# Shorter stages for the second layer's weight sums and a wider spread of the next token sums

## The chip, the cores and the metric

The kernel runs on one core of one Trainium2 chip. The core has TensorE (PE, the products; PEld is its weight load), VectorE (DVE), ScalarE (ACT), GpSimd (POOL) and SyncE (SP, which issues all DMAs here from one queue). Each engine works through its own queue in order. The metric is the time of one execution on the device in microseconds, the median of several runs.

## The reference, cut to what matters

Attention over four batches with eight heads (576 tokens, 64 wide), mixed with a memory read-out, gives 2304 tokens of 512 values. Two feed-forward layers follow, with 512 x 2048 weights in and 2048 x 512 out:

```python
x = attn_out.transpose(0, 2, 1, 3).reshape(B * S, H * D)
h = x @ w1_in;  x = (h * np.cos(h)) @ w1_out                            # layer one
h = x @ w2_in;  x = (h * np.tanh(np.log1p(np.exp(h)))) @ w2_out         # layer two
```

The weights come as 64-bit floats and are taken apart on the chip.

## The kernel before, in words

Every factor of the feed-forward products is split into a high and a low half in the fast 32-bit format, and a product is three matmuls: high by high, high by low, low by high.

The work runs in these stages. **Attention** (0 to about 395 us) goes through 80 steps (16 head pairs of 5 row blocks); each step has parts a, b and c, and the main loop (L840) hangs other work behind part a. **Layer one, first half** of the hidden units, runs beside attention in blocks of 256 tokens and on to about 490 us; **its second half** (`m2`, L875) runs in blocks of 512 tokens from about 490 to 690 us: 72 yields, each about twelve products of 512 columns. The chain of the cosine there goes from PE over ACT (L380), DVE (L381), ACT (L385), DVE (L388), ACT (the high half) to POOL (the low half, L398), whose result PE needs for the products of L492.

**Layer two** (`strassen_ffn`, from about 690 us) uses Strassen's scheme: seven products of sums of blocks in place of eight. It runs over 3 token blocks of 768 and, in each, over 8 groups of 256 hidden units, 24 groups in all. A group has 84 matmuls of 384 columns: 42 for the first products (`product`, L750: the seven of `PROD`) and 42 for the second products (L725), which belong to the pair of groups two earlier and go in the order of `LAST`. A group's sums are DVE's (L649, L644), the activation is ACT's (L653), the high halves are ACT's and the low halves POOL's (`halves`, L656 to L662). After the last pair of a token block, `done` (L670) forms the outputs from the seven accumulators, alternating DVE and POOL (L684), and stores them.

What layer two needs is prepared elsewhere:

- *Weight sums* (`strassen_weights`, L532). For a group, two raw pieces are fetched and converted (L143 to L146), four sums are formed on POOL (L544), and four results are split on ACT and on DVE or POOL in turn (L547, L548) and stored to DRAM (L549): 2 loads and 4 stores in SP's queue. The eight groups of the weight in are made beside attention from step 33 on (`SUM0`, `SUMR`), the eight of the weight out beside `m2`, one raw piece in four yields. The four results of a group have four buffers, `ws0`, `ws2`, `ws3`, `ws5`, one each.
- *Token sums* (`strassen_x`, L562). A token block needs seven sums of its four quarters, split. For the first block they are made beside `m2`; for the others inside `strassen_ffn`: at the end of group 6 the four loads, two differences and two of the seven splits, and in group 7 the rest, one part after each product (`coming`). DVE does differences and splits (L576, L583, L593, L598), ACT the high halves (L575).

The order on each engine comes from a planner with a model of times; `tc.issue_after(x)` keeps what is issued inside from being placed ahead of instruction x.

Of the kernel before, what the change touches and what calls it, by code (L numbers as in the profile page):

```python
# [20 lines left out]
BUFS = dict(  # L21
    mb=2, kd=4, qd=3, aD=4, vt=2, qt=1, ph=2, den=2, mo=4, xH=1, xL=3, sm=7, mn=2, at=8, aT=7, u=2, e=3, g=4, h=4, y=4, xb=3, xbH=4, xbL=4, yp=3, wst=4, S=6, T=8, sw=1, ws=1, wq=10, xr=4, xt=2, xc=9, xc0=2, us=14, g3=17, y3=6, h3=2, w2=8, ac=14,
)
# [4 lines left out]
SUM0 = 36  # L28
SUMR = 0.4
# [11 lines left out]
    wh="ap", aT="av", yl="p", ml="p", y0="v", y1="a", aD="v", y3="a", yf="vp", x3l="v", x3l0="pv", x3d0="p", x3d="v", ws4="p", ws2="a", wh2="a",  # L41
# [8 lines left out]
def attention_moe_moe_kernel(  # L50
# [140 lines left out]
    def attention(ap, pools):  # L191
# [46 lines left out]
        def stage_a(b, p, i):  # L238
# [37 lines left out]
            nc.vector.reciprocal(sm, sm)  # L276
            for j, at in enumerate(ats):
                turn_of("sc", b == 0).tensor_scalar(at[:, :N], at[:, :N], sm[:, j:j + 1], gates[j], ALU.mult, ALU.mult)  # L278
# [242 lines left out]
    LAST = "A11 A12 S2 S3 A22 S1 S4".split()  # L521
# [10 lines left out]
    def strassen_weights(srcs, order, dst):  # L532

        pc = []
        for n, t in enumerate(ahead(srcs), -AHEAD):
            if t is not None:
                pc.append(t.rearrange(f"p ({order}) -> p h c f", c=2, h=2))
            if len(pc) == 2:
                (a11, a21), (a12, a22) = [[q[:, h] for h in range(2)] for q in pc]
                sw = wk.tile([P, 4, 2, P], F32, tag="sw", name="sw", bufs=BUFS["sw"])  # L540
                s1, s2, s3, s4 = [sw[:, k] for k in range(4)]
                for d, x, y, op in ((s1, a21, a22, ALU.add), (s2, s1, a11, ALU.subtract),
                                    (s3, a11, a21, ALU.subtract), (s4, a12, s2, ALU.subtract)):
                    turn_of("ws4").tensor_tensor(d, x, y, op)  # L544
                for k0, k1, t in ((0, 2, pc[1]), (2, 3, pc[0][:, 0:1]), (3, 5, sw[:, :2]), (5, 7, sw[:, 2:])):
                    ws = wk.tile([P, k1 - k0, 2, 2, P], F32R, tag=f"ws{k0}", name="ws", bufs=BUFS["ws"])
                    scaled("wh2", ws[:, :, 0], t)  # L547
                    turn_of("w2l").tensor_tensor(ws[:, :, 1], t, ws[:, :, 0].bitcast(F32), ALU.subtract)  # L548
                    nc.sync.dma_start(dst[n // 2, :, k0:k1], ws.rearrange("p k l c f -> p k (l c f)").bitcast(F32))  # L549
                pc = []  # L550
            yield n + 1

    def strassen_in(win):
        wi = win.bitcast(I32).rearrange("(c p) (f two) -> p c f two", p=P, two=2)
        return strassen_weights([wi[:, c:c + 2, f:f + 2 * P, :] for f in range(0, DFF, 2 * P) for c in range(0, NC, 2)],
                                "c h f", wsD)

    def strassen_out(wout):
        wo = wout.bitcast(I32).rearrange("(f p) (e two) -> p f e two", p=P, two=2)
        return strassen_weights([wo[:, f] for f in range(DFF // P)], "h c f", woD)  # L560

    def strassen_x(t0, out, store=False):  # L562
# [22 lines left out]

        halves("A11", b11)
        t1 = diff(b12, b11)
        t2 = diff(b22, t1)
        halves("S2", t2)
# [3 lines left out]
        turn_of("x3d" + u).tensor_tensor(b12, b22, b12, ALU.subtract)  # L593
        halves("S3", b12)
# [3 lines left out]
        turn_of("x3d" + u).tensor_tensor(b21, b21, t2, ALU.subtract)  # L598
        halves("A22", b21)
        yield  # L600
        halves("S4", b22)

# [20 lines left out]
    def strassen_ffn(pool, xs, w, fill):  # L623
# [9 lines left out]
        g3 = wk.tile([P, BUFS["g3"], 2, TS], F32R, name="g3")  # L633
# [8 lines left out]
        def sub(x, y, out=None):  # L642
            out = cell() if out is None else out
            marks['v'] = nc.vector.tensor_tensor(out, x, y, ALU.subtract).ins  # L644
            return out
# [10 lines left out]
        def halves(k, name, x):  # L656
            slot = free.pop(0)
            t = g3[:, slot]
            scaled("mh", t[:, 0], x)
            ins = turn_of("ml").tensor_tensor(t[:, 1], x, t[:, 0].bitcast(F32), ALU.subtract).ins  # L660
            marks['p' if ins.engine == mybir.EngineType.Pool else 'v'] = ins
            g[k, name] = slot, t  # L662
# [7 lines left out]
        def done(k0, name, c, y):  # L670
# [3 lines left out]
            if tl == 0:  # L674
                a = acc[name, c] = ring(wk, "ac", [P, TS])
                scaled("y3", a, y)
                return
# [21 lines left out]
            elif name == "S2":  # L699
                pre("S3", a)  # L700
                pre("S4", a)
            elif name == "S3":
                pre("A22", a, ALU.subtract)
            elif name == "A22":
                store(a, 1, 0)
            elif name == "S1":
                pre("S4", a)
                turn_of("yf").tensor_tensor(a, a, acc["S3", c], ALU.add)
                store(a, 1, 1)
            else:  # L710
                store(a, 0, 1)

        def last_products():
            for i in range(2):
                fetch_last(i)
            for i, (k0, name) in enumerate(chain):
# [26 lines left out]
        for k in range(n + KS):  # L743
            nw = {}

            def product(b, name, first):
# [8 lines left out]
                with behind():  # L755
# [216 lines left out]
```

## Time and profile before

| what | value |
|---|---|
| median of 3 runs | 1070.65 us (1068.82 to 1073.72) |
| the profiled execution | 1071.4 us |
| its span, first to last instruction | 1069.5 us |
| mean granted TensorE clock | 0.983 |
| instructions | 19321 |

The profile is one execution. The views used below give, for a stretch of the span, how long each engine was busy and with how many instructions; for one line, its count and mean duration; and, in order of time, what ended the idle time before an instruction. A stretch in which PE runs fewer matmuls of one size than elsewhere is a stretch in which it waited.

### The profile page before, as it was taken

To read this page: it belongs to the slowest core of one execution; us is meant where nothing else is said; L and a number is where in the kernel's file an instruction comes from. 1 tells how busy PE (TensorE), PEld (TensorE's weight loads), DVE (VectorE), ACT (ScalarE), POOL (GpSimd) and SP (SyncE) were. 2 spreads that over 40 slices of the span, in tenths; PEclk is the share of its full clock that TensorE was granted. 3 is DMA by queue.
4 is the path that set the end of the run, shared out by engine and by line. 5 is a ranking of instruction groups with operands and counts; after the bars stand their busy time and mean duration, and the time that the engine had idled before them with its cause. 6 is when DMAs were issued, how large, how long until landed. Compare 5 with 4: busy or idle time off the path is not lost.

```text
span 1069.5 us, 19321 instructions
## 1 busy us (share of the span) xinstructions
PE 1021.0 (95%) x6704; PEld 901.6 (84%) x6704; DVE 704.2 (66%) x1442; ACT 580.7 (54%) x1274; POOL 597.1 (56%) x581
## 2 busy tenths in 40 slices
PE   6988999998999999999999999999989999899996
PEld 4665678886878889998887888999989999799996
DVE  3689876658566645886584784454688466973666
ACT  5787676867575743334464564554443644545441
POOL 3378736555455524654575776554547545665555
PEclk8999899999999999999999999999999999999998
DMA  7367636646552337424586798987588958687781
GB/s 251 131 215 260 191 131 199 240 160 240 177 180 107 108 118 265 151 99 128 162 296 223 273 364 314 393 296 259 198 276 260 329 205 271 218 297 254 248 288 59
DMA packets 121840, 236.18 MB, mean 221 GB/s; under 512 B 11920, under 2 KB 35984, under 8 KB 121744
## 3 DMA queue, kind: packets, MB, share of 16 engines
q1 hardware_dynamic: 121744, 234.95, 63.9%
q8 instruction: 54, 0.88, 0.3%
q14 instruction: 42, 0.34, 0.1%
HBM read 176.44 MB, written 58.46 MB: 220 GB/s over the span
## 4 chain that ended last, share of the span: by engine, by line
PE 71%; DVE 13%; DMA 6%; ACT 3%; POOL 3%; issue 3%; SPq 1%; POOLq 0%; DVEq 0%; ACTq 0%
PE h L426 16%; PE y L492 16%; PE y L725 12%; PE h L750 12%; PE o L337 5%; PE sp L251 4%; PE tp L310 3%; DVE wst L146 2%; PE o L326 1%; DMA w<-woD 1%; DMA xbH<-xsH 1%; DVE wst L145 1%; DVE us L644 1%; PE mp L290 1%; DVE xc L576 1%
## 5 line engine op out<-in xcount | busy, mean ns | idle before, releaser
L660 POOL TENSOR_TENSOR g<-us,g 128x384 fp32r<-128x384 f32 x168 | 186.1, 1128 | 144.5 <-ACT g L129 48.7
L492 PE MATMUL y<-g,w 128*128 128x256 f32 (+1 forms) x1344 | 223.9, 319 | 1.2 <-POOL g L398 1.2
L492 PEld LDWEIGHTS y<-g,w 128*128 128x128 f32 x1344 | 193.0, 192 | 28.0 <-issue 10.9
L426 PE MATMUL h<-xbH,w 128*128 128x256 f32 (+1 forms) x896 | 208.5, 318 | 0.7 <-DMA xbH<-xsH 0.7
L725 PE MATMUL y<-g,w 128*128 128x384 f32 x1008 | 199.2, 339 | 7.2 <-DMA w<-woD 3.2
L750 PE MATMUL h<-xc,wq 128*128 128x384 f32 x1008 | 197.4, 336 | 7.4 <-DVE us L649 6.0
L725 PEld LDWEIGHTS y<-g,w 128*128 128x128 f32 x1008 | 178.0, 190 | 12.1 <-DMA w<-woD 6.6
L750 PEld LDWEIGHTS h<-xc,wq 128*128 128x128 f32 x1008 | 176.5, 188 | 10.3 <-DVE us L649 7.9
L426 PEld LDWEIGHTS h<-xbH,w 128*128 128x128 f32 x896 | 151.5, 191 | 13.8 <-DMA xbH<-xsH 1.1
L398 POOL TENSOR_TENSOR g<-u,g 128x512 fp32r<-128x512 f32 x72 | 108.4, 1521 | 82.7 <-DVE g L131 54.4
L278 POOL TENSOR_SCALAR at<-at,sm,omg 128x128 f32<-128x128 f32 (+2 forms) x144 | 109.4, 769 | 73.6 <-DVE sm L276 45.8
L649 DVE TENSOR_TENSOR us<-h,us 128x384 f32<-128x384 f32 x120 | 66.4, 554 | 114.5 <-PE h L750 105.8
L426 PE MATMUL h<-xbL,w 128*128 128x256 f32 (+1 forms) x448 | 141.3, 315 | 0.0
L129 ACT ACTIVATE g<-us 128x384 fp32r<-128x384 f32 x168 | 86.6, 525 | 40.0 <-DVE us L644 37.6
L653 ACT ACTIVATE us<-us 128x384 f32<-128x384 f32 x72 | 37.9, 526 | 113.8 <-DVE us L649 107.1
L426 PEld LDWEIGHTS h<-xbL,w 128*128 128x128 f32 x448 | 85.8, 192 | 5.4 <-issue 0.3
L380 ACT ACTIVATE u<-h 128x512 int32<-128x512 f32 x72 | 42.5, 594 | 80.8 <-PE h L426 76.7
L256 ACT ACTIVATE at<-at,mn 128x128 f32<-128x128 f32 (+3 forms) x128 | 71.2, 557 | 24.0 <-DVE mn L253 22.5
L644 DVE TENSOR_TENSOR us<-us 128x384 f32<-128x384 f32 x96 | 74.8, 814 | 11.8 <-ACT us L653 9.5
L146 DVE SCALAR_TENSOR_TENSOR wst<-wst 128x512 int32<-128x512 int32 x64 | 79.2, 1247 | 0.2
L381 DVE SCALAR_TENSOR_TENSOR u<-u,h 128x512 f32<-128x512 int32 x72 | 48.4, 681 | 46.8 <-ACT u L380 46.4
L310 PE MATMUL tp<-ident,at 128*128 128x128 f32 x384 | 66.1, 289 | 9.1 <-POOL at L278 6.8
(103 smaller groups left out, 1505.2 us busy)
## 6 DMA issues: line engine op xcount, KB each, us to landing
wq<-wsD SPq DMA_DIRECT2D x168, 256.0 KB, 4.7
w<-woD SPq DMA_DIRECT2D x168, 256.0 KB, 4.9
wsD<-ws SPq DMA_DIRECT2D x24, 512.0 KB, 5.4
woD<-ws SPq DMA_DIRECT2D x24, 512.0 KB, 6.3
wst<-in_w1i_dram SPq DMA_DIRECT2D x16, 512.0 KB, 4.5
wst<-in_w1o_dram SPq DMA_DIRECT2D x16, 512.0 KB, 4.9
wst<-in_w2i_dram SPq DMA_DIRECT2D x16, 512.0 KB, 4.7
wst<-in_w2o_dram SPq DMA_DIRECT2D x16, 512.0 KB, 5.1
```

The lines of the kernel that those rows point to most:

```text
L129: eng.activation(dst, src, AF.Copy, scale=scale)
L146: nc.vector.scalar_tensor_tensor(lo, hi, 3, lo, ALU.logical_shift_left, ALU.bitwise_or)
L256: marks["act"] = nc.scalar.activation(at[:, :N], at[:, :N], AF.Exp, bias=mn[:, j:j + 1], scale=-1.0, accum_out=sm[:, j:j + 1]).ins
L278: turn_of("sc", b == 0).tensor_scalar(at[:, :N], at[:, :N], sm[:, j:j + 1], gates[j], ALU.mult, ALU.mult)
L310: nc.tensor.transpose(tp[:, c:c + P], at[:, c:c + P], ident)
L398: turn_of(kind).tensor_tensor(gL, g, gH.bitcast(F32), ALU.subtract)
L426: nc.tensor.matmul(h[:, a * T:(a + 1) * T], w_[:, c, f0:f0 + P], x_[c], start=m == 0, stop=m == 3 * NC - 1)
L492: nc.tensor.matmul(y[e // per][:, cols], w_[:, f, es], g_, start=fst and m == 0 and e % per == 0, stop=lst and m == 2, skip_group_check=True)
L644: marks['v'] = nc.vector.tensor_tensor(out, x, y, ALU.subtract).ins
L660: ins = turn_of("ml").tensor_tensor(t[:, 1], x, t[:, 0].bitcast(F32), ALU.subtract).ins
L725: nc.tensor.matmul(y, w_[:, wl, c], x[:, xl], start=m == 0, stop=m == 3 * KS - 1, skip_group_check=True)
L750: nc.tensor.matmul(b, w[name][:, wl, c], x[name][:, xl, c], start=first and m == 0, stop=m == 5, skip_group_check=True)
```

## The change

1. The weight sums go in stages. `strassen_weights` now stops after each fetch ahead, each converted raw piece, each two of the four sums, and each stored result: eight stages a group. The main loop takes one stage in each attention step from step 29 on (51 stages: three fetches and six groups), behind the step's exponential, its scaling on POOL and its reciprocal on DVE. The other ten groups (two of the weight in, eight of the weight out) go beside `m2`, once the conversion of layer one's weights is over: two stages a yield, one in each third.
2. The four result buffers become one ring of two, `ws`. The token ring `xc` has ten buffers, not nine.
3. `strassen_x` stops after every difference and split, twelve steps; in `strassen_ffn` it begins behind group 3 of a token block and takes its steps at the places in `STEPS` (group counted from the block's end, product), the loads first.
4. Layer two's second products go in the order A11, A12, S4, S1, S2, S3, A22, and `done` combines them accordingly; the subtractions for S3 and A22 go to POOL in all groups but the last, whose low halves alternate between DVE and POOL (`mz`); `h3` has three PSUM banks, `y3` five; operand slots and accumulators are tiles of their own; the first weights of the second products are fetched behind group 0.

```diff
-    ... ws=1, xc=9, y3=6, h3=2 ...
+    ... ws=2, xc=10, y3=5, h3=3 ...
-SUM0 = 36
-SUMR = 0.4
+SUM0 = 32
+SUMS = 6
+SUM2 = 3
...
-            nc.vector.reciprocal(sm, sm)
+            marks["vec"] = nc.vector.reciprocal(sm, sm).ins
...
+    STEPS = [(-4, 4), (-3, 2), (-3, 4), (-3, 6), (-2, 1), (-2, 3), (-2, 5), (-2, 6), (-1, 1), (-1, 2), (-1, 3), (-1, 5)]
-    LAST = "A11 A12 S2 S3 A22 S1 S4".split()
+    LAST = "A11 A12 S4 S1 S2 S3 A22".split()
...
+    def strassen_weights(pieces):
+        raws = ahead([src for srcs, _, _ in pieces for src in srcs])
+        for _ in range(AHEAD):
+            next(raws)
+            yield
+        for _, order, dst in pieces:
+            pc = []
+            for _ in range(2):
+                pc.append(next(raws).rearrange(f"p ({order}) -> p h c f", c=2, h=2))
+                yield
...
+                turn_of("ws4").tensor_tensor(d, x, y, op)
+                if i % 2:
+                    yield
+            for k0, k1, t in ((0, 2, pc[1]), (2, 3, pc[0][:, 0:1]), (3, 5, sw[:, :2]), (5, 7, sw[:, 2:])):
+                ws = wk.tile([P, 2, 2, 2, P], F32R, tag="ws", name="ws", bufs=BUFS["ws"])[:, :k1 - k0]
+                scaled("wh2", ws[:, :, 0], t)
+                turn_of("w2l").tensor_tensor(ws[:, :, 1], t, ws[:, :, 0].bitcast(F32), ALU.subtract)
+                nc.sync.dma_start(dst[:, k0:k1], ws.rearrange("p k l c f -> p k (l c f)").bitcast(F32))
+                yield
...
             elif name == "S2":
                 pre("S3", a)
+                turn_of("yf").tensor_tensor(a, a, acc["S1", c], ALU.add)
                 pre("S4", a)
+                store(acc["S4", c], 0, 1)
             elif name == "S3":
                 pre("A22", a, ALU.subtract)
+                pre("S1", a)
+                store(acc["S1", c], 1, 1)
             elif name == "A22":
                 store(a, 1, 0)
...
+            if k == 1:
+                next(lasts)
...
-                with behind():
-                    next(coming, None)
+                j = PROD.index(name)
+                for a in range(STEPS.count((groups[k][1] - ng, j))):
+                    with behind():
+                        next(coming, None)
...
-                halves(k, "S3", sub(r22, r12, r12))
-                halves(k, "A22", sub(t2, r21, r21))
+                halves(k, "S3", sub(r22, r12, r12, k + 1 == n))
+                halves(k, "A22", sub(t2, r21, r21, k + 1 == n))
-                if groups[k][1] == ng - 2 and k + 2 < n:
+                if groups[k][1] == ng // 2 - 1 and k + ng < n:
...
         if kind == "a" and s >= SUM0 - AHEAD:
-            with tc.issue_after(marks["act"]):
-                while summed < min(s - SUM0 + 1 if s < SUM0 else int((s - SUM0 + 1) * SUMR), DFF // P):
-                    summed = next(gi)
+            with tc.issue_after(marks["act"]), tc.issue_after(marks["pool"]), tc.issue_after(marks["vec"]):
+                next(gi, None)
...
-            if i % 4 == 1:
+            if done_b == 4 * NTL - 1:
                 with tc.issue_after(marks["cos"]), tc.issue_after(last_sin[0]):
-                    next(gc, None)
-            if i >= XSUM0 and i % 4 == 3:
+                    for _ in range(1 if i % SUM2 == 0 else 2):
+                        next(gc, None)
+            if i >= XSUM0 and i % 2 == 1:
```

## Rows read from the trace of the kernel before

**Rows 1.** The page's first part: busy us, share of span, instructions.
```profile
PE 1021.0 (95%) x6704; PEld 901.6 (84%) x6704; DVE 704.2 (66%) x1442; ACT 580.7 (54%) x1274; POOL 597.1 (56%) x581
```

**Rows 2.** Busy us (instructions) by stretch, then PE clock, DMA share, GB/s.
```profile
775.00:850.00 75.00, 69.93 (x384) 67.61 (x383) 53.30 (x83) 35.70 (x70) 43.38 (x38) 0.98 0.87 298
850.00:900.00 50.00, 50.00 (x291) 50.00 (x290) 30.11 (x51) 23.02 (x47) 28.59 (x27) 1.00 0.66 218
900.00:975.00 75.00, 69.88 (x383) 65.74 (x382) 53.31 (x82) 34.90 (x69) 44.28 (x38) 1.00 0.79 267
```

**Rows 3.** Timeline, first block change: start, us, instructions, [idle before <-releaser].
```profile
786.25 1.76 DVE L576 TENSOR_TENSOR xc<-xr,xc 128x768 fp32r<-128x768 f32 x1
...
788.06 2.37 PE L725 MATMUL y<-g,w 128*128 128x384 f32 x12 [1.14 <-DMA w<-woD]
...
799.07 1.38 PE L750 MATMUL h<-xc,wq 128*128 128x384 f32 x6 [2.22 <-DVE us L649]
```

**Rows 4.** Timeline, the end of the span.
```profile
1051.20 0.96 PE L725 MATMUL y<-g,w 128*128 128x384 f32 x4 [2.01 <-POOL g L660]
...
1052.77 10.16 PE L725 MATMUL y<-g,w 128*128 128x384 f32 x48 [0.60 <-ACT g L129]
...
1065.09 1.01 DVE L690 TENSOR_TENSOR ac<-y,ac 128x384 f32<-128x384 f32 x2
```

**Rows 5.** Busy time by stretch, beside attention.
```profile
250.00:275.00 25.00, 21.81 (x184) 18.05 (x185) 20.19 (x54) 19.04 (x48) 16.57 (x20) 1.00 0.64 226
300.00:325.00 25.00, 21.48 (x166) 16.56 (x166) 18.47 (x56) 19.28 (x48) 12.87 (x16) 0.93 0.63 220
```

**Rows 6.** Timeline beside attention, one wait of PE.
```profile
264.42 0.66 ACT L144 ACTIVATE wst<-wst 128x512 int32<-128x512 uint32 x1
...
265.39 0.65 PE L337 MATMUL o<-aT,vt 128*64 128x128 f32 x6 [1.81 <-ACT aT L129]
```

**Rows 7.** Busy time by stretch, layer one's second half and after.
```profile
521.00:590.00 69.00, 68.34 (x302) 56.27 (x301) 45.00 (x57) 36.30 (x60) 43.30 (x37) 1.00 0.72 250
590.00:654.00 64.00, 64.00 (x284) 52.98 (x283) 48.13 (x51) 38.17 (x61) 48.04 (x35) 1.00 0.83 308
654.00:700.00 46.00, 46.00 (x309) 43.80 (x308) 23.29 (x34) 23.43 (x40) 25.19 (x23) 1.00 0.95 358
```

**Rows 8.** Groups by line: total busy us, mean ns | idle before, releasers.
```profile
L660 POOL TENSOR_TENSOR g<-us,g 128x384 fp32r<-128x384 f32 x168 | 186.1, 1128 | 144.5 <-ACT g L129 48.7 <-PE y L725 39.7 <-issue 32.1
...
L644 DVE TENSOR_TENSOR us<-us 128x384 f32<-128x384 f32 x96 | 74.8, 814 | 11.8 <-ACT us L653 9.5 <-DMA wq<-wsD 0.6
...
L684 POOL TENSOR_TENSOR ac<-ac 128x384 f32<-128x384 f32 x15 | 20.8, 1399 | 16.5 <-DVE ac L690 15.0 <-PE h L750 1.3
```

**Rows 9.** Raw weights, 480 to 700 us: ns min/median/max, first, last start.
```profile
L145 DVE SCALAR_TENSOR_TENSOR wst<-wst x21: 678/683/2340, 485.3 to 673.6; 128x512 int32<-128x512 int32 x21
L146 DVE SCALAR_TENSOR_TENSOR wst<-wst x21: 675/1666/2343, 487.6 to 674.3; 128x512 int32<-128x512 int32 x21
...
L129 ACT ACTIVATE wst<-wst x16: 654/664/675, 504.0 to 671.3; 128x512 f32<-128x512 f32 x16
L544 POOL TENSOR_TENSOR sw<-wst x16: 844/856/1322, 509.3 to 677.1; 128x256 f32<-128x256 f32 x16
```

**Rows 10.** Busy time of instructions on the finished weight sums alone.
```profile
500.00:690.00 190.00, 16.96 (x16) 18.84 (x32) 18.65 (x16) 1.00 0.76 278
```

**Rows 11.** Waits of SP's queue: total us, times, longest.
```profile
SPq L549 <- POOL ws L548: 91.5, 25, 17.7
```

**Rows 12.** DMA issues: count, KB each, median us from issue to landing.
```profile
woD<-ws SPq DMA_DIRECT2D x24, 512.0 KB, 6.3
...
xr<-ysF SPq DMA_DIRECT2D x12, 384.0 KB, 5.7
```

**Rows 13.** Timeline, end of one cosine chain.
```profile
608.02 3.72 POOL L398 TENSOR_TENSOR g<-u,g 128x512 fp32r<-128x512 f32 x2
...
612.75 4.70 PE L492 MATMUL y<-g,w 128*128 128x512 f32 x20
```

More of the change, by code (lines that the diff above doesn't have):

```diff
@@ L530, in ahead @@
             yield to_f32(raw.pop(i), "ws2") if i >= 0 else None
[L532 to L551, printed above, removed]
@@ L553, in strassen_in, with strassen_pieces @@
-    def strassen_in(win):
+    def strassen_pieces(win, wout):
         wi = win.bitcast(I32).rearrange("(c p) (f two) -> p c f two", p=P, two=2)
-        return strassen_weights([wi[:, c:c + 2, f:f + 2 * P, :] for f in range(0, DFF, 2 * P) for c in range(0, NC, 2)],
-                                "c h f", wsD)
-    def strassen_out(wout):
         wo = wout.bitcast(I32).rearrange("(f p) (e two) -> p f e two", p=P, two=2)
-        return strassen_weights([wo[:, f] for f in range(DFF // P)], "h c f", woD)
+        n = DFF // (2 * P)
+        return ([([wi[:, c:c + 2, tl * 2 * P:(tl + 1) * 2 * P, :] for c in range(0, NC, 2)], "c h f", wsD[tl])
+                 for tl in range(n)] +
+                [([wo[:, f] for f in (2 * tl, 2 * tl + 1)], "h c f", woD[tl]) for tl in range(n)])
@@ L601, in strassen_x @@
         halves("S4", b22)
+        yield
     def load_w(tl, n, tag="wq", src=wsD):
@@ L632, in strassen_ffn @@
         chain = [(k, name) for k in range(0, n, KS) for name in LAST]
-        g3 = wk.tile([P, BUFS["g3"], 2, TS], F32R, name="g3")
+        g3 = [wk.tile([P, 2, TS], F32R, tag=f"g3{i}", name="g3", bufs=1) for i in range(BUFS["g3"])]
+        sums = [wk.tile([P, TS], F32, tag=f"ac{i}", name="ac", bufs=1) for i in range(14)]
         free = list(range(BUFS["g3"]))
@@ L640, in cell, with sub @@
             return wk.tile([P, TS], F32, tag="us", name="us", bufs=BUFS["us"])
-        def sub(x, y, out=None):
-            out = cell() if out is None else out
-            marks['v'] = nc.vector.tensor_tensor(out, x, y, ALU.subtract).ins
+        def sub(x, y, out=None, vector=True):
+            if out is None:
+                out = cell()
+            if vector:
+                marks['v'] = nc.vector.tensor_tensor(out, x, y, ALU.subtract).ins
+            else:
+                marks['p'] = nc.gpsimd.tensor_tensor(out, x, y, ALU.subtract).ins
             return out
@@ L657, in halves @@
             slot = free.pop(0)
-            t = g3[:, slot]
+            t = g3[slot]
             scaled("mh", t[:, 0], x)
-            ins = turn_of("ml").tensor_tensor(t[:, 1], x, t[:, 0].bitcast(F32), ALU.subtract).ins
+            ins = turn_of("ml" if k + 1 < n else "mz").tensor_tensor(t[:, 1], x, t[:, 0].bitcast(F32), ALU.subtract).ins
             marks['p' if ins.engine == mybir.EngineType.Pool else 'v'] = ins
@@ L674, in done @@
             if tl == 0:
-                a = acc[name, c] = ring(wk, "ac", [P, TS])
+                a = acc[name, c] = sums[LAST.index(name) + 7 * c]
                 scaled("y3", a, y)
@@ L792, in strassen_ffn @@
                 halves(k, "S2", t2)
-                halves(k, "S3", sub(r22, r12, r12))
-                halves(k, "A22", sub(t2, r21, r21))
+                halves(k, "S3", sub(r22, r12, r12, k + 1 == n))
+                halves(k, "A22", sub(t2, r21, r21, k + 1 == n))
                 w = nw
-                if groups[k][1] == ng - 2 and k + 2 < n:
-                    nt = groups[k + 2][0]
+                if groups[k][1] == ng // 2 - 1 and k + ng < n:
+                    nt = groups[k + ng][0]
                     xs[nt] = {}
                     coming = strassen_x(nt, xs[nt])
-                    with behind():
-                        next(coming)
             between(k, 1)
```

35 lines of the change are left out of this document (20 added, 15 removed).

## The prediction

> **What bounds the kernel now.** I read the page's busy times first. TensorE (PE) is busy 95% of the span [rows 1], so the most that any reordering can win is PE's idle time, 1069.5 - 1021.0 = 48.5 us; the products themselves are untouched. So I went to the busy times by stretch, to see where PE idles. In the last stage the undisturbed middle of a token block shows 291 products in 50 us, one each 0.172 us, with PE busy throughout; the two stretches around a change of token block show 384 and 383 in 75 us, where that pace gives 436 [rows 2]. That is 52 and 53 products short, 9.0 and 9.2 us. DVE is the busiest of the side engines there (53.3 of 75 us against 30.1 of 50).
>
> The timeline of the first block change says why [rows 3]. All arithmetic for the next block's token sums falls into one group of 84 products (14.4 us). DVE's long operations on 768 elements (1.76 us) stand ahead of the short sums that release PE's accumulators; PE then waits 2.22 us for DVE, and 1.14 us for a weight load, which shares SP's queue with the four token loads, 384 KB each [rows 12], of this step.
>
> At the end, PE waits 2.01 and 0.60 us for the low and high halves of the last group, finishes at 1062.93, and the last two sums on DVE start at 1065.09; the span ends at 1069.5 [rows 4].
>
> Beside attention the stretches 250 to 275 and 300 to 325 us leave PE idle 3.2 and 3.5 us [rows 5]; in one such wait (1.81 us) ACT converts a raw weight piece ahead of the copy that PE needs [rows 6]. In the stage of layer one's second half (521 to 654 us) PE idles only 0.7 us, although DVE and POOL are 75% busy in its second half [rows 7].
>
> **The change part by part.** *Token sums over four groups.* Twelve steps in place of six; the same seven splits and four differences, no operation more. The four loads of 384 KB go out in group 4 of the block, not at the end of group 6; splits and differences follow in groups 5, 6, 7. Those eleven operations of DVE, at up to 1.76 us [rows 3], come to as much as 19 us against one group's 14.4; now three or four of them fall in a group, at most 7.0 us. The steady group leaves DVE 40% idle (30.1 of 50 us [rows 2]), 5.7 us of 14.4, and loses two subtractions (1.6 us) besides: they fit. If that cover were gone, the cost would be today's 18.2 us. I leave 1.8 us per block change for a weight load behind four token loads (today 1.14 us) and the final accumulator sums, and take 18.2 - 3.6 = 14.6 us saved; bounds 5 (half the wait is DMA and accumulator sums) and 18.2.
>
> *Two subtractions of each group (but the last) on POOL.* 23 x 2 = 46 leave DVE at 0.81 us and cost POOL about what a low half does, 1.13 us [rows 8]. POOL then has nine operations, 10.2 us of 14.4: hidden, since the two results are now consumed last. In the two groups after a block change it also has seven accumulator sums at 1.40 us: 2 x 10.2 + 9.8 = 30.2 of 28.8 us, over by 1.4. Its cover is the idle rest of the following group (4.2 us); if that fails, PE waits about 1.4 us twice. Inside the 3.6 left above.
>
> *New order of the last products, 3 banks for first products and 5 for second.* First products no longer wait for the previous group's last bank; second ones have one bank less to wait in, six products' time (1.03 us) of slack. A11, A12, S4 are ready before the last sums S1, S2, S3, A22, so at the end 3 x 12 products (6.2 us) stand between the last first-layer product and the late operands: the waits of 2.01 and 0.60 us go. Low halves of the last group alternate over DVE and POOL. Gain 2.6 us; bounds 0 and 2.6.
>
> *After PE's last product* the old order leaves DVE 2.2 us late (1065.09 against 1062.93). In the new one only A22's sum and store follow; its partner is formed from S3 two products earlier, but S2 now brings three sums, not two, so I take 1.9 us of the 6.6 us; bounds 0 (those sums queue instead) and 2.2.
>
> *Weight sums beside attention.* Six groups in 51 stages, one per step, where eight went by raw pieces, every second one with a whole group's sums behind it. Two groups leave: 12 DMA issues on SP, and about 5 us of ACT, 7 of DVE, 6 of POOL each (below). The stages stand behind the step's scaling and reciprocal. But a raw conversion is one stage as before, so a wait as in [rows 6] can recur, 12 times in place of 16. Of 6.7 us I take 2; bounds 0 and 6.7.
>
> *Ten groups beside the following stage.* Its products run one per 0.225 us (284 in 64 us [rows 7]); a step of twelve is 2.70 us. Before, one raw piece per four steps: a group each 21.6 us. Now 5 stages per 3 steps: one each 1.62 us, a group of eight each 13.0 us. A group costs DVE 2 x (0.68 + 1.67) + 16.96/8 = 6.8 us, POOL up to 4 x 0.86 + 18.65/8 = 5.8 us, ACT 2 x (0.66 + 0.66) + 18.84/8 = 5.0 us [rows 6, 9, 10]. In 590 to 654 us that is 4.9 groups, not 3.0: DVE 48.1 + 13 = 61 of 64 us, POOL 48.0 + 11 = 59, ACT 38 + 10 = 48. DMA adds 1.9 x 2.9 MB, about 87 GB/s, to 308, more than the 358 that the next stretch reaches at a share of 0.95; the sums will lag. Nothing waits for them before group 6 of the last stage, but in-order queues pass their lateness on. SP already stands 91.5 us behind POOL's halves with its stores [rows 11]; behind those stand the block loads. Lower bound 0 (PE idled nothing at 75%), upper the second rival's 30 us. Nearest is the row of 0.66 us idle in 521 to 590; I take four such waits, 2.6 us.
>
> *Costed at nothing:* splitting the operand and accumulator tiles (same slots, same reuse order; a false wait could only go), the early fetch of two second-layer operands at group 1 (hidden by 14 us of products; uncovered one load), one more token buffer, paid for by the smaller ring of weight sums.
>
> **Sum.** The profiled execution took 1071.4 us, 1.9 around its span. 1071.4 - 14.6 - 2.6 - 1.9 - 2.0 + 2.6 = 1052.9. It stood 0.75 above the median shown, so 1052.2: forecast 1052.
>
> **Rivals.** *Ring of two holds ACT (slower).* Before, four tags held a group's four sums. Now two slots serve; a slot is taken for a copy of 0.6, a low half of 1.2 and a store of 6.3 us to landing [rows 12], 8.1 us. The group's third copy comes two stages (3.2 us) after the first. Where the written order puts it there, ACT stands 4.9 us at the head of its queue, with the cosine chain behind it. That chain has 1.0 us to spare (POOL's halves end at 611.74, PE's run starts at 612.75 [rows 13]); with what else is idle, 3 us a group, 30 us in ten: 1080. It decides above 2.1 us a group, where all 21 us gained are gone. For it: slot time is 2.5 times the spacing. Against: the next four stages need no slot, a group needs 16 us of the ring against 13 offered, and the order can put the copy later. Chance 0.11.
>
> *DVE and POOL become the bound in 590 to 654 us.* 61 and 59 of 64 us leave nothing for inflation, and DVE's second merge of a raw piece ranges from 0.68 to 2.34 us [rows 9]. If five groups' ten merges ran 0.7 us longer, that stretch would grow by some 7 us: 1059. Against: the sums may spill past 654 us. Chance 0.15.
> On such overlaps the Trainium skill (SBUF — State Buffer, section Who interferes with whom) says that a DVE instruction with two SBUF inputs and a GpSimd instruction reading SBUF exclude each other for the whole instruction. The spread of that merge agrees; by the rule the denser schedule turns into blocked time, which is this rival.
>
> *Block changes keep half their wait,* through loads, POOL's 30.2 of 28.8 us and the fifth bank: 9.1 us back and not 14.6: 1058. Chance 0.10.
>
> *The spreading does nothing,* because the copies of block sums still wait for old buffers and fall into group 7 (four of seven must): about 1067. One spare buffer more and DVE's idle 40% speak against. Chance 0.05.
>
> The forecast itself (1046 to 1060) has 0.59. A difference under 0.5%, 5.4 us, is about what this kernel's measurement cannot tell. Faster: forecast and the 1059 and 1058 cases but for their tails, 0.78; same 0.12; slower 0.10. All gains at their bounds at once give 1041; the range begins a little above, at 1043, and ends at 1068, past the rivals that only shrink the gain; what it leaves out is mostly the ring's 1080.
>
> **What would show it.** Right: about 430 products in each 75 us around the block changes, no wait of PE on DVE's sums above 1 us; no wait ahead of the last 60 products; DVE's last sum about 1 us after PE; sums still running past 660 us with PE idle under 4 us from 521 to 700. Wrong: ACT waiting for a store's landing at the weight sums' copies; PE waiting on POOL's halves between 540 and 680 us; PE short again where POOL does the accumulator sums.

## The result, and the profile after

The kernel after takes 1059.63 us, median of 4 runs (1057.27 to 1062.88), against 1071.04 us for the kernel before, median of 4 (1068.82 to 1073.72). The ratio is 0.9894, with a 95% interval of [0.9859, 0.9929]: 11.4 us, or 1.1%, faster. Of the kernel after, the execution with the profile took 1057.27 us (span 1055.5), the quickest of its four, so the two profiles lie 14.0 us of span apart, not 11.4.

The busy times of the page show the same work as [rows 1], with 30.7 us less of DVE and 37.6 us more of POOL:

```profile
PE 1017.3 (96%) x6704; PEld 897.9 (85%) x6704; DVE 673.5 (64%) x1400; ACT 576.1 (55%) x1274; POOL 634.7 (60%) x623
```

Busy time by stretch, kernel after. The columns are PE, PEld, DVE, ACT and POOL, each with its instructions, then granted clock, DMA share and GB/s; the first five rows are stretches of [rows 2, 7], the last four those of the next fence.

```profile
521.00:590.00 69.00, 68.43 (x302) 56.36 (x302) 49.95 (x62) 41.17 (x69) 45.77 (x39) 1.00 0.79 276
590.00:654.00 64.00, 61.11 (x267) 49.61 (x266) 48.51 (x53) 39.51 (x66) 46.84 (x33) 1.00 0.88 314
654.00:700.00 46.00, 44.99 (x302) 42.59 (x301) 22.94 (x33) 20.50 (x35) 22.85 (x22) 1.00 1.02 385
775.00:850.00 75.00, 72.83 (x419) 72.22 (x418) 47.23 (x74) 35.72 (x73) 53.71 (x48) 1.00 0.80 261
900.00:975.00 75.00, 74.61 (x430) 73.99 (x429) 45.31 (x70) 38.11 (x78) 57.71 (x53) 1.00 0.80 263
...
250.00:350.00 100.00, 99.69 (x808) 79.69 (x807) 61.24 (x190) 65.11 (x161) 43.94 (x53) 1.00 0.45 147
500.00:675.00 175.00, 171.54 (x790) 142.53 (x789) 116.42 (x137) 91.76 (x152) 111.06 (x87) 1.00 0.76 274
675.00:740.00 65.00, 60.65 (x376) 58.48 (x376) 32.14 (x47) 41.11 (x83) 51.12 (x50) 1.00 0.85 310
740.00:1020.00 280.00, 277.45 (x1596) 276.16 (x1595) 170.70 (x271) 130.59 (x264) 200.31 (x182) 1.00 0.83 280
```

The same view of the kernel before, in the last four stretches:

```profile
250.00:350.00 100.00, 93.28 (x750) 77.25 (x751) 65.22 (x182) 62.99 (x158) 51.41 (x60) 0.97 0.52 177
500.00:675.00 175.00, 174.34 (x806) 145.55 (x806) 115.85 (x138) 94.60 (x154) 111.50 (x87) 1.00 0.74 268
675.00:740.00 65.00, 63.30 (x399) 62.53 (x398) 29.51 (x48) 35.28 (x71) 35.27 (x33) 1.00 0.85 300
740.00:1020.00 280.00, 269.81 (x1516) 263.36 (x1515) 184.80 (x296) 128.42 (x258) 158.86 (x140) 0.99 0.77 260
```

Read row by row they say where the time came from. From 740 to 1020 us, layer two proper, PE runs 1596 products in place of 1516: 80 more, 13.7 us at 0.172 us each [rows 2]. Beside attention PE's idle time falls from 6.7 to 0.3 us in 100. Two stretches lose: 500 to 675 us is 2.8 us shorter of PE time, and 675 to 740 us, the start of layer two, 2.65 us.

How far layer two has come at 740 us, by the products of its two kinds alone (PE and PEld; first the two rows of the kernel before, L750 and L725, then those of the kernel after, L771 and L744):

```profile
0.00:740.00 740.00, 33.83 (x174) 30.02 (x174) 0.98 0.61 210
0.00:740.00 740.00, 20.52 (x109) 19.08 (x110) 0.98 0.61 210
...
0.00:740.00 740.00, 35.35 (x185) 32.05 (x186) 0.98 0.60 207
0.00:740.00 740.00, 16.86 (x84) 14.52 (x84) 0.98 0.60 207
```

That is 283 products before and 269 after: at 740 us the kernel after is 14 products, 2.4 us, behind. What it wins beside attention has been lost again by then, and the whole gain lies in layer two behind 740 us.

The timeline of the kernel after at its remaining waits (start, us, instructions, idle before):

```profile
610.08 2.81 PE L494 MATMUL y<-g,w 128*128 128x512 f32 x11 [1.15 <-POOL g L400]
...
620.96 3.28 PE L494 MATMUL y<-g,w 128*128 128x512 f32 x13 [1.74 <-POOL g L400]
...
721.39 0.43 ACT L130 ACTIVATE ws<-wst 128x256 fp32r<-128x256 f32 x1
722.38 1.15 DVE L566 TENSOR_TENSOR ws<-sw,ws 128x512 fp32r<-128x512 f32 x1 [2.43 <-ACT ws L130]
725.00 0.47 ACT L786 ACTIVATE us<-h 128x384 f32<-128x384 f32 x1
725.52 4.44 PE L771 MATMUL h<-xc,wq 128*128 128x384 f32 x24 [2.47 <-ACT us L786]
...
1038.71 3.39 PE L744 MATMUL y<-g,w 128*128 128x384 f32 x16 [0.32 <-ACT g L130]
1042.51 5.85 PE L744 MATMUL y<-g,w 128*128 128x384 f32 x32 [0.41 <-DVE g L680]
1048.52 3.78 POOL L704 TENSOR_TENSOR ac<-ac 128x384 f32<-128x384 f32 x3 [0.49 <-DVE ac L721]
1051.56 0.56 DVE L710 TENSOR_TENSOR ac<-ac,y 128x384 f32<-128x384 f32 x1
```

The waits at 610 and 621 us are for POOL's low halves of the cosine chain. At 721 us weight sums are still being made: ACT's work at 721.39 and DVE's operation at 722.38, which waits 2.43 us for ACT, belong to them, and both stand in their queues ahead of the activation that PE waits 2.47 us for. The waits at the end are 0.73 us, not 2.61 [rows 4]. PE ends at about 1048.4 us, and 7.1 us remain to the end of the span (6.6 before).

The waits of ACT from 500 to 740 us, kernel after (total us, times, longest), hold two that the ring of two causes; each ends when a store of finished sums has landed:

```profile
ACT ws L130 <- DMA woD<-ws: 12.8, 7, 3.0
...
ACT ws L130 <- DMA wsD<-ws: 4.0, 3, 2.8
```

### The profile page after: what moved, and what is told of

Same layout as the page of the kernel before. It is cut to its first block, busy times and chain, and to the rows that moved or that the text cites. A ratio compares the mean times of both kernels' runs of the same rounds, so it can differ in the third digit from the quotient of the medians.

```text
span 1055.5 us, 19374 instructions
## 1 busy us (share of the span) xinstructions
PE 1017.3 (96%) x6704; PEld 897.9 (85%) x6704; DVE 673.5 (64%) x1400; ACT 576.1 (55%) x1274; POOL 634.7 (60%) x623
## 4 chain that ended last, share of the span: by engine, by line
PE 67%; DMA 9%; DVE 9%; ACT 6%; POOL 4%; issue 4%; SPq 1%; POOLq 0%; ACTq 0%; DVEq 0%
PE y L744 15%; PE h L771 15%; PE h L428 12%; PE y L494 11%; PE o L339 4%; PE sp L252 4%; PE tp L312 3%; DMA wst<-in_w1i_dram 2%; DMA wst<-in_w1o_dram 2%; PE o L328 1%; DVE wst L146 1%; DMA w<-woD 1%; DMA wsD<-ws 1%; POOL at L279 1%; DMA woD<-ws 1%
## 5 line engine op out<-in xcount | busy, mean ns | idle before, releaser
L680 POOL TENSOR_TENSOR g<-us,g 128x384 fp32r<-128x384 f32 x164 | 177.3, 1099 | 74.2 <-ACT g L130 73.0
L494 PEld LDWEIGHTS y<-g,w 128*128 128x128 f32 x1344 | 191.3, 190 | 33.5 <-issue 10.3
L744 PE MATMUL y<-g,w 128*128 128x384 f32 x1008 | 196.2, 336 | 4.0 <-DMA w<-woD 2.5
L771 PE MATMUL h<-xc,wq 128*128 128x384 f32 x1008 | 195.7, 335 | 2.6 <-ACT us L786 2.5
L279 POOL TENSOR_SCALAR at<-at,sm,omg 128x128 f32<-128x128 f32 (+2 forms) x144 | 114.3, 802 | 115.2 <-DVE sm L277 68.0
L744 PEld LDWEIGHTS y<-g,w 128*128 128x128 f32 x1008 | 175.9, 188 | 7.2 <-DMA w<-woD 2.4
L771 PEld LDWEIGHTS h<-xc,wq 128*128 128x128 f32 x1008 | 176.2, 188 | 3.4 <-ACT us L786 2.8
L400 POOL TENSOR_TENSOR g<-u,g 128x512 fp32r<-128x512 f32 x72 | 103.3, 1449 | 111.7 <-ACT g L130 54.5
L428 PEld LDWEIGHTS h<-xbH,w 128*128 128x128 f32 x896 | 151.3, 192 | 12.9 <-DMA xbH<-xsH 1.0
L669 DVE TENSOR_TENSOR us<-h,us 128x384 f32<-128x384 f32 x120 | 66.3, 554 | 109.6 <-PE h L771 78.7
L673 ACT ACTIVATE us<-us 128x384 f32<-128x384 f32 x72 | 37.6, 524 | 96.1 <-DVE us L669 96.1
L710 DVE TENSOR_TENSOR ac<-y,ac 128x384 f32<-128x384 f32 x120 | 63.8, 550 | 22.1 <-PE y L744 21.7
L254 DVE CUSTOM_DVE_ANT_0 at<-sp,mask 128x128 f32<-128x128 f32 (+3 forms) x128 | 59.5, 483 | 25.5 <-PE sp L252 20.5
```

Of the source, the lines that this page charges most:

```text
L279: marks["pool"] = turn_of("sc", b == 0).tensor_scalar(at[:, :N], at[:, :N], sm[:, j:j + 1], gates[j], ALU.mult, ALU.mult).ins
L400: turn_of(kind).tensor_tensor(gL, g, gH.bitcast(F32), ALU.subtract)
L428: nc.tensor.matmul(h[:, a * T:(a + 1) * T], w_[:, c, f0:f0 + P], x_[c], start=m == 0, stop=m == 3 * NC - 1)
L494: nc.tensor.matmul(y[e // per][:, cols], w_[:, f, es], g_, start=fst and m == 0 and e % per == 0, stop=lst and m == 2, skip_group_check=True)
L669: marks['v'] = nc.vector.tensor_tensor(c, b, x, ALU.add).ins
L680: ins = turn_of("ml" if k + 1 < n else "mz").tensor_tensor(t[:, 1], x, t[:, 0].bitcast(F32), ALU.subtract).ins
```

## The experiments

Each ratio is the kernel's time over that of the kernel before, on the same chip (its medians there lay at 1073.1 to 1073.8 us), with its 95% interval. The kernel after stands at 0.9894 [0.9859, 0.9929]; it was not run again beside the experiments, so they are compared with it by these ratios. "Products" are those between 740 and 1020 us, with 1516 before and 1596 after, in one profiled execution of each kernel.

**Everything but the spreading.** The token sums go back into one group; the rest of the change stays.

```diff
-    STEPS = [(-4, 4), (-3, 2), (-3, 4), (-3, 6), (-2, 1), (-2, 3), (-2, 5), (-2, 6), (-1, 1), ...
+    STEPS = [(-1, 0), (-1, 1), (-1, 1), (-1, 1), (-1, 2), (-1, 3), (-1, 4)]
...
-                if groups[k][1] == ng // 2 - 1 and k + ng < n:
+                if groups[k][1] == ng - 2 and k + 2 < n:
...
+                        for _ in range(5):
+                            next(coming)
```

> The changed kernel with the token sums put back: they begin behind group 6 of a token block and all fall between there and product 4 of group 7; the rest stays changed. Theory A (what was won in layer two came from spreading DVE's long operations over four groups): the 14 us at the two block changes come back, 1073 us (1069 to 1077), with PE some 45 products short in each stretch around a block change. Rival (the order of the second products, the banks and the subtractions on POOL had already taken the pressure off): 1060 to 1063 us.

1065.55 us, 0.9936 [0.9906, 0.9966]; 1545 products, 51 fewer than after but 29 more than before. The time lies between the two branches, and its interval overlaps with that of the kernel after; the loss shows in the products.

**The spreading alone,** in the kernel before.

```diff
-    ... yp=3, ... xc=9 ...
+    ... yp=2, ... xc=10 ...
+    STEPS = [(-4, 4), (-3, 2), ...]
...
+                j = PROD.index(name)
+                for a in range(STEPS.count((groups[k][1] - ng, j))):
...
-                if groups[k][1] == ng - 2 and k + 2 < n:
+                if groups[k][1] == ng // 2 - 1 and k + ng < n:
```

> The kernel before, with the spread of the token sums alone (STEPS, ten token buffers; to make room, two buffers for layer one's outputs in place of three). Theory A: the block changes give their 14 us, 1057 us (1054 to 1061). Rival (the spread needs the new order and banks with it): 1066 us or more.

1068.93 us, 0.9965 [0.9940, 0.9991]; 1546 products. Spreading alone brings 30 of the 80. Around both runs the windows and, at the block change of this one, the timeline:

```profile
740.00:1020.00 280.00, 271.91 (x1545) 266.80 (x1544) 172.71 (x263) 128.35 (x258) 191.70 (x177) 1.00 0.79 263
```
```profile
740.00:1020.00 280.00, 272.88 (x1546) 268.67 (x1545) 191.53 (x302) 130.19 (x264) 162.47 (x143) 0.99 0.79 267
```
```profile
803.35 2.90 PE L758 MATMUL h<-xc,wq 128*128 128x384 f32 x9 [1.86 <-DVE us L657]
```

The first row is everything but the spreading, the second the spreading alone, the third its timeline. L657 there is the sum of [rows 3]: PE still waits 1.86 us for DVE, where it waited 2.22 us. A spread of the long operations has not taken that wait away.

**The banks.** The kernel after with two banks for first products and six for second, as before; nothing else is undone.

```diff
-    ... y3=5, h3=3 ...
+    ... y3=6, h3=2 ...
```

> The changed kernel with two banks for first and six for second products, as before; order, subtractions on POOL and all else changed. If the banks carry what the third part is worth (about 10 us by its undoing): 1066 us or more, with PE's waits of 1 to 2 us for DVE's accumulator sums back at 24 products into a group. If order and subtractions carry it: within 3 us of the changed kernel.

1072.51 us, 1.0000 [0.9979, 1.0021]; 1538 products. Two numbers take the whole gain back. The window and the timeline of the second block change:

```profile
740.00:1020.00 280.00, 270.02 (x1538) 265.63 (x1537) 172.03 (x261) 127.39 (x258) 190.14 (x174) 1.00 0.78 261
```
```profile
926.70 2.35 PE L771 MATMUL h<-xc,wq 128*128 128x384 f32 x12 [1.84 <-DVE us L669]
```

A first product is back to waiting 1.84 us for DVE's sum, in spite of the spread; the kernel after has no wait on L669 in the whole stretch. The waits of PE from 740 to 1020 us (total us, times, longest), in this order: the kernel before, everything but the spreading, the spreading alone, two and six banks (two rows), the kernel after:

```profile
PE h L750 <- DVE us L649: 5.5, 3, 2.2
...
PE h L771 <- DVE us L669: 3.8, 5, 1.1
...
PE h L758 <- DVE us L657: 2.7, 2, 1.9
...
PE h L771 <- DVE us L669: 5.0, 4, 1.8
PE y L744 <- DMA w<-woD: 4.7, 5, 2.0
...
PE y L744 <- DMA w<-woD: 2.5, 2, 2.1
```

With two banks PE also waits 2.2 us more for weight loads than in the kernel after; why these come later there is not shown. So the third bank does not add to the spreading: it carries it. The spread makes DVE's sums less late, and the bank covers what lateness stays. Without the bank the spread gives 22 to 30 products; the bank without the spread 29; the two together 80.

**The order of the last products.** First the whole group of edits to them undone (order, `done`, subtractions on DVE, low halves on POOL, and banks six and two), then the order and `done` alone.

```diff
-    ... y3=5, h3=3 ...
+    ... y3=6, h3=2 ...
-    LAST = "A11 A12 S4 S1 S2 S3 A22".split()
+    LAST = "A11 A12 S2 S3 A22 S1 S4".split()
...
-                halves(k, "S3", sub(r22, r12, r12, k + 1 == n))
-                halves(k, "A22", sub(t2, r21, r21, k + 1 == n))
+                halves(k, "S3", sub(r22, r12, r12))
+                halves(k, "A22", sub(t2, r21, r21))
```

> The changed kernel with the third part of the change undone: the old order of the second products and its sums, all subtractions on DVE, the last low halves on POOL, two banks for first and six for second products; spread token sums and short stages stay. If the third part gives at the block changes what the spread leaves (some 5 us) and 2.5 us at the end: 7 us more than the changed kernel, with PE's shortfall at the block changes as with the spread alone (about 10 us) and 15.4 us from the last first-layer product to PE's end, not 12.9. If the parts do not add: within 3 us of the changed kernel.

1073.09 us, 0.9995 [0.9970, 1.0020]; 1543 products: the same as the banks alone, and more than either branch expected. The subtractions on POOL and the order add nothing that shows beside the banks.

```diff
-    LAST = "A11 A12 S4 S1 S2 S3 A22".split()
+    LAST = "A11 A12 S2 S3 A22 S1 S4".split()
...
```

> The changed kernel with the old order of the second products and the old combination of the outputs; banks, subtractions on POOL, alternating last low halves and all else changed. If the order carries the third part: PE waits again for S2's and S3's operands at the end (2 us) and behind each pair of groups, 1066 us or more. If the banks carry it: 1060 to 1063 us, with 1 to 2.5 us of it at the end.

1061.46 us, 0.9906 [0.9870, 0.9943]; 1590 products. From the last first-layer product to PE's end it takes 14.3 us, against 12.9 after and 15.4 before; from there to the end of the span 6.5 against 7.1. What the order buys is 1.4 us ahead of PE's end, and it gives 0.6 back behind it: too little for this measurement.

**S2 before S1,** to shorten what follows PE's last product.

```diff
-    LAST = "A11 A12 S4 S1 S2 S3 A22".split()
+    LAST = "A11 A12 S4 S2 S1 S3 A22".split()
...
-                turn_of("yf").tensor_tensor(a, a, acc["S1", c], ALU.add)
+                pre("S4", a)
+            elif name == "S1":
```

> The changed kernel with the second products in the order A11, A12, S4, S2, S1, S3, A22: S2's three sums become two and S1 brings one, so that the last three names bring three sums each half and not five. If POOL's three sums of 1.3 us after PE's end (3.8 us in one run) set the end: from PE's last product to the span's end 5 us in place of 7.1, 2 us less in all. Rival: the last store sets it, 7.1 us stay; or S2's operand, now wanted one name earlier, makes PE wait before the last products, 1 to 2 us.

1061.37 us, 0.9899 [0.9866, 0.9932]: no difference from after, and in its profile 8.4 us behind PE's end in place of 7.1. It did not shorten the end.

**A ring of four for the weight sums.**

```diff
-    ... ws=2 ...
+    ... ws=4 ...
```

> The changed kernel with four slots for finished weight sums in place of two. Theory B (the ring of two holds ACT and drags the sums past the start of layer two): the sums end before 700 us and not at 743, the wait of 2.5 us at the start of layer two goes, and part of the 4 us beside layer one: 1055 us (1053 to 1058). Rival (the density on DVE and POOL is what costs): the sums pack closer, 1060 to 1064 us.

1065.24 us, 0.9926 [0.9896, 0.9956]: no faster; by the medians slower, with intervals that overlap. The stores of the weight out's sums, first to last (kernel after, then this one), and two windows and one wait of this one:

```profile
L567 SPq DMA_DIRECT2D woD<-ws x32: 319/326/1550, 561.9 to 742.8; - x32
```
```profile
L567 SPq DMA_DIRECT2D woD<-ws x32: 319/320/488, 560.1 to 683.6; - x32
```
```profile
500.00:675.00 175.00, 167.22 (x751) 137.43 (x750) 125.65 (x144) 99.18 (x165) 127.32 (x100) 0.99 0.79 287
675.00:740.00 65.00, 63.81 (x404) 62.41 (x403) 23.60 (x38) 33.12 (x64) 34.73 (x33) 1.00 0.84 311
```
```profile
662.73 5.57 PE L494 MATMUL y<-g,w 128*128 128x512 f32 x17 [3.75 <-POOL g L400]
```

The ring of two does hold ACT, and it paces the sums: a group takes (742.8 - 561.9) / 31 x 4 = 23.3 us, against 15.9 with four buffers. Freed of it the sums end 59 us earlier and layer two's start gets 3.2 us back, but the denser sums cost 4.3 us of PE from 500 to 675 us, where PE now waits 3.75 us at once for POOL. Here the ring worked as a brake on the dense run. That is read from one profile; in time the two kernels cannot be told apart.

**An even pace.** The ten groups start with the first yield of layer one's second half, one stage a yield and a second one in each sixth, not five stages per three yields once the conversion of the weights is over.

```diff
-            if done_b == 4 * NTL - 1:
-                with tc.issue_after(marks["cos"]), tc.issue_after(last_sin[0]):
-                    for _ in range(1 if i % SUM2 == 0 else 2):
-                        next(gc, None)
+            with tc.issue_after(marks["cos"]), tc.issue_after(last_sin[0]):
+                for _ in range(2 if i % 6 == 0 else 1):
+                    next(gc, None)
```

> The changed kernel with the stages of the ten groups spread evenly over layer one's second half from its first yield (one a yield, two in each sixth), in place of five per three yields after the weight conversion. Theory C (what is lost from 600 to 625 us is the density of the weight sums on DVE and POOL): PE's two waits of 1.2 and 1.7 us for POOL's low halves there go, about 4 us less from the stage, against some us at the start of layer two where sums still run. Rival D (single long token sums of the first block, 2.6 and 2.4 us on POOL, stand between two low halves that PE needs): the waits stay, within 2 us of the changed kernel.

1051.36 us, 0.9806 [0.9767, 0.9844]: the fastest of all, and clear of the kernel after (0.9894 [0.9859, 0.9929]). Its windows, one wait, and what ACT waited for at the copies of the weight sums (total us, times):

```profile
500.00:675.00 175.00, 170.61 (x792) 141.40 (x792) 115.49 (x142) 95.61 (x158) 111.58 (x92) 1.00 0.78 282
675.00:740.00 65.00, 64.94 (x404) 64.62 (x404) 30.44 (x45) 37.74 (x78) 51.76 (x50) 1.00 1.03 375
740.00:1020.00 280.00, 278.59 (x1607) 278.15 (x1606) 179.57 (x276) 132.78 (x268) 202.43 (x184) 1.00 0.81 269
```
```profile
526.58 0.50 PE L428 MATMUL h<-xbH,w 128*128 128x512 f32 x1 [1.44 <-DVE u L390]
```
```profile
  DMA woD<-ws: 29.3, 13
  DMA wsD<-ws: 5.6, 4
```

The waits at 610 and 621 us are gone, but others for the same chain came at 527 and 569 us (1.44 and 1.69), so the second half of layer one gains nothing (170.61 against 171.54 us). The gain shows at the start of layer two, where 64.94 of 65 us are busy (4.3 us), and after it (11 products, 1.9 us). The two profiles differ by 9.9 us. Of these 2.4 us lie ahead of the store of attention's 6th head pair (129.9 against 132.3 us), where the edit changes nothing; from there to the first 300 products of layer two this kernel takes 607.5 us against 613.1, and it wins 1.9 us behind them. So the even pace is worth some 7 us here, not all of the difference. The ring of two holds ACT for 34.9 us in it, against 16.8 after: a wait of ACT for the ring is not in itself what PE pays for.

**The first token block's sums all on DVE,** to clear POOL ahead of the two waits.

```diff
-    ... x3l0="pv", x3d0="p" ...
+    ... x3l0="v", x3d0="v" ...
```

> The changed kernel with the first block's token sums (differences, low halves) on DVE alone in place of POOL or both in turn. Theory D: PE's waits of 1.2 and 1.7 us for POOL's low halves between 600 and 625 us go, 3 to 4 us less from the stage. Theory C: DVE takes the density over, PE idles as much or more there.

1055.19 us, 0.9842 [0.9804, 0.9880]. The timeline at the place:

```profile
615.80 0.67 ACT L130 ACTIVATE ws<-wst 128x512 fp32r<-128x512 f32 x1 [5.50 <-DMA woD<-ws]
...
619.99 0.79 PE L428 MATMUL h<-xbH,w 128*128 128x512 f32 x1 [3.16 <-DVE u L390]
```

PE still waits, and longer: 3.16 us, for the cosine chain at DVE, behind an ACT that the ring has held 5.50 us. Token sums on POOL did not make these waits. The start of layer two is better (64.70 of 65 us busy), but 500 to 675 us is worse (168.90 against 171.54), and the profiled execution is no shorter than that of the kernel after (span 1056.5 against 1055.5). The lower median, with an interval that overlaps with after's, shows no gain.

**Attention.** Seven groups beside it and nine later; six groups, but each group's sums in one lump; and seven together with the even pace.

```diff
-SUMS = 6
+SUMS = 7
...
-                next(gi, None)
+                for _ in range(2 if s % 6 == 1 else 1):
+                    next(gi, None)
```

> The changed kernel with seven groups of weight sums beside attention in 59 stages (two in one step of six), nine beside layer one's second half. If the density beside layer one's second half is what costs: 1057 to 1058 us. If taking two groups away was what freed attention (4.7 us earlier at its end): attention ends 2 us later again and the sum is 1060 to 1062 us. If the short stages freed it, attention ends where it does now.

```diff
-                next(gi, None)
+                for _ in range(1 if s < SUM0 else (1, 0, 0, 0, 7, 0, 0, 0)[(s - SUM0) % 8]):
+                    next(gi, None)
```

> The changed kernel with the six groups beside attention taken in lumps: of a group's eight stages one in one step and seven four steps later, none in the others. If the short stages freed attention: pairs 6 to 16 take 266 us again, not 259, and the whole is some 6 us slower. If fewer groups, or their place behind POOL's scaling and DVE's reciprocal, freed it: 259 us, no difference.

```diff
-SUMS = 6
+SUMS = 7
...
+                for _ in range(2 if s % 6 == 1 else 1):
+                    next(gi, None)
...
-            if done_b == 4 * NTL - 1:
...
+                for _ in range(2 if i % 18 == 0 else 1):
+                    next(gc, None)
```

> The changed kernel with seven groups beside attention in short stages and nine beside layer one's second half at an even pace from its first yield (one stage a yield, two in each eighteenth). By the density theory both steps take load from the crowded stretch, and attention does not pay for the seventh group: 2 to 4 us under the even pace alone, about 1048 us. If the even pace had already removed all that the density costs: 1051 us as with it alone.

1058.39 us, 0.9885 [0.9826, 0.9943]; 1060.09 us, 0.9902 [0.9869, 0.9935]; 1053.48 us, 0.9842 [0.9815, 0.9868]. One group more beside attention shows no gain, with the even pace or without; the 1048 us expected of the two together did not come. The same stretch of seven groups, then of the lumps:

```profile
250.00:350.00 100.00, 99.41 (x838) 81.94 (x838) 61.30 (x198) 64.22 (x167) 51.67 (x60) 1.00 0.48 161
```
```profile
250.00:350.00 100.00, 98.52 (x831) 81.21 (x830) 62.56 (x193) 65.61 (x163) 45.21 (x54) 1.00 0.42 142
```

Both keep most of the gain over 93.28 us. So it is neither the shortness of the stages nor the step from seven groups to six.

## Why the prediction was right or wrong

The forecast was 1052 us in 1043 to 1068; 1059.63 us lies in the range, 7.6 us above the forecast. In the profiles the account is closer, since that of after took 1057.27 us. Part of that is luck: attention won 5.2 us more than forecast, and the stage behind it lost about as much more.

| step | forecast | measured |
|---|---|---|
| block changes of layer two | -14.6 | -13.7 |
| waits at the end | -2.6 | -1.9 |
| after PE's last product | -1.9 | +0.5 |
| attention | -2.0 | -7.2 |
| beside layer one's second half | +2.6 | +2.8 |
| start of layer two | none | +2.65 |
| sum | -18.5 | -16.9 |

Attention is measured from the store of the 6th head pair to that of the 16th and last (266.1 us before, 258.9 after). That is two single executions, but the kernel with only the spreading has 267.6, and every kernel with six or seven groups there 257.4 to 259.0. Up to either mark PE has done as many products before as after.

The table's rows are idle times and windows fixed in time, and its sum is 2.9 us more than the 14.0 us by which the profiles differ. Counted by work done, in the order in which layer two's 2016 products start, the account closes. After the first 300 PE starts the next at 743.1 us before and at 745.4 us after, after 1800 at 1020.6 and 1009.1, and the spans end at 1069.5 and 1055.5: 2.3 us lost ahead of layer two's steady run, 13.8 won at the block changes, 2.5 won at the end. At attention's first mark the kernel after is 2.5 us late already (132.3 against 129.8 us; its variants with the same stages up to there have 129.9 to 134.8, so that is scatter). From that mark to the first 300 products the two take 613.3 and 613.1 us: the shorter stages of the weight sums won nothing on balance.

**Block changes: the size was right by luck, the step that carried it was not.** The prediction laid all of the 14.6 us to "token sums over four groups" and gave the new split of banks no price there ("six products' time" of slack). Spreading alone measured 30 products, 5.2 us, in place of 14.6, and the banks undone alone brought the time back to 1.0000. The step that failed is the reading of [rows 3]: the wait of 2.22 us was laid to the long operations ahead of DVE's short sums. It has a second condition, that only two banks stand between that sum and PE's next first product, and with three the sum may come that much later. Either half alone leaves waits of 1 to 1.9 us. That the bank is needed is shown by the two-and-six run; that the two together give more than their sum rests on product counts (80 against 51 to 59), which lie at 1574 to 1611 in the eight experiments that keep both. The rivals "spreading does nothing" and "half the wait stays" come closest to the kernel with two banks.

**The two subtractions on POOL** hid as forecast: no wait of PE on a low half of layer two from 740 to 1020 us. They gave no time that shows.

**The end.** The waits fell to 0.73 us, near the forecast, and a spell of half clock behind them went too (last section). Behind PE the lower bound came out ("these sums queue instead") and a little worse: 3.78 us of three sums on POOL stand between, and the reordering by hand did not mend it.

**Attention** gave more than its upper bound of 6.7 us, which counted idle time alone: two spells of half clock behind such waits (last section) went with them. The mechanism named, conversions ahead of the copy that PE needs, fits: the waits of [rows 6], 5.6 us of them on ACT between 250 and 350 us before, are not in that stretch after. What took them away is left open: lumps and seven groups keep the gain, so by exclusion the place of the stages, behind POOL's scaling and DVE's reciprocal, is the candidate; that was not isolated. A rival is untested: before, a group took five steps (0.4 raw pieces a step, two a group), and in all these kernels it takes about seven or eight.

**Ten groups beside layer one.** The term of 2.6 us was too small. The windows show 2.8 us up to 675 us and 2.65 at the start of layer two; counted by work it is 7.9, since a lead of 5.6 us after 2200 of layer one's 2688 products (592.9 against 598.5 us) has become the lag of 2.3. Idle times miss part of it: a single product of 512 columns is shown busy for 0.50 us where in a run the next follows after 0.225. The picture was wrong too. A group was to take 13.0 us and DVE to be busy 61 of 64 us from 590 to 654 us; a group of the weight out took 23.3 us and DVE was busy 48.5. The ring of two held ACT 16.8 us in all, as that rival said, but the waits slowed the sums more than they stopped PE: the even pace has 34.9 us of them and is the fastest. A long one can hold PE, as the 5.50 us with the first block's sums on DVE do (3.16 us). The ring's rival fails in its price (PE idled 2.8 us more, not 30), and the rival of a bound on DVE and POOL is what a larger ring brings part of. What I missed is where the lateness went: "the sums will lag" was priced at nothing behind 690 us, because nothing needs them before group 6. They do not delay what needs them but what shares their queues: ACT and DVE at 721 us. The even pace shows that this start is worth 4.3 us.

## What to carry to other kernels

A long operation ahead of a short one and a scarce accumulator bank are one wait with two conditions: price them together, and try each with and without the other, since either alone can look worthless. Work that nothing needs yet still costs where its queue is shared; ask what it will stand ahead of when it is late. Of three ways to fit it in here, an early, even pace beat the dense run and the dense run with a larger ring. And a gain in one stage can be lost in the next: count the work done at a few marks, not idle time in fixed windows alone.

## What the hardware showed that I had not expected

A wait of PE can cost more than its length. Behind waits of 1.01, 2.22 and 1.80 us, and behind those of 2.01 and 0.60 us at the end, the matmuls of the next 3.4 us ran at a granted clock of about half, near the lower of the two levels (1.2 and 2.4 GHz). Before, in four places:

```profile
312.00:315.40 3.40, 3.40 (x18) 3.06 (x19) 0.86 (x5) 2.01 (x9) 3.40 (x5) 0.52 0.99 367
...
800.00:803.40 3.40, 3.40 (x13) 3.23 (x12) 3.40 (x6) 2.13 (x4) 2.50 (x2) 0.53 0.44 127
...
326.00:329.40 3.40, 3.40 (x19) 3.40 (x18) 2.93 (x10) 2.65 (x10) 3.09 (x3) 0.53 0.00 0
...
1052.80:1056.20 3.40, 3.40 (x11) 3.40 (x12) 2.03 (x3) 0.91 (x2) 3.40 (x4) 0.50 0.29 103
```

Each such spell costs some 3.4 x 0.47 = 1.6 us in which PE counts as busy, so it is missing from a sum of idle times. From 740 to 1020 us PE's idle time fell by 7.6 us and its products rose by 13.7 us' worth; one spell lies there before and none after, which explains 1.6 of the 6.1 us between. A part more is in the reading: a product of 384 columns is shown busy for 0.33 us, the next one starts 0.17 us after it, so each of the 13 waits there (2 after) hides up to 0.16 us. The rest is not placed. The wait of 1.86 us with the spreading alone has one behind it too (0.57 from 803.3 to 806.7 us); the wait of 2.47 us at 725 us after has none that shows in its stretch's mean of 1.00. I have not found what decides it.
